# Large buffers moved to multiples of 4 KB, and one projection moved ahead in the tail

## The chip, the core and the metric

The kernel runs on one core of one Trainium2 chip. The core has five engines with an instruction stream each: TensorE (PE, with its weight loads shown as PEld), VectorE (DVE), ScalarE (ACT), GpSimd (POOL) and SyncE (SP), and 16 DMA engines that move data between HBM and the on-chip memory SBUF. SBUF has 128 partitions; a tile takes the same byte range in each of them, so a tile has one start address that holds in every partition. The metric is the device time of one execution in microseconds; less is better.

## What is computed

One step of decoding for a batch of 4: attention over a cache of 4,096 keys and values in 32 heads, a feed-forward block (GEGLU) beside it on the same input, and a gate that mixes the two. All data are float32.

```python
def _A_ref(x, k_cache, v_cache, wq, wo):        # x (4, 1, 512), caches (4, 32, 4096, 128)
    q = (x @ wq).reshape(B, Sq, H, Dh).transpose(0, 2, 1, 3)
    scores = jnp.einsum("bhqd,bhkd->bhqk", q, k_cache) * (Dh ** -0.5)
    p = _softmax(scores, axis=-1)
    o = jnp.einsum("bhqk,bhkd->bhqd", p, v_cache)
    return o.transpose(0, 2, 1, 3).reshape(B, Sq, H * Dh) @ wo      # wo (4096, 512)

def _B_ref(x, w_gate, w_up, w_down):            # (512, 1792), (512, 1792), (1792, 512)
    return (_gelu(x @ w_gate) * (x @ w_up)) @ w_down

g = _sigmoid((x * gate_w).sum(-1, keepdims=True))
return g * a + (1 - g) * b
```

The two caches are 268 MB each; every byte of them is read once.

## The kernel before

**Tiles.** The caches are cut into 64 tiles each (`NT`): tile i holds two heads of one batch, as 128 partitions of 64 keys (or values) of 128 numbers, which is a row of 32,768 bytes in each partition and 4 MB in all. The function `load` issues one DMA from SyncE for a tile (the last V tile in two halves). All large inputs pass through one pool `kv` of five buffers of that size: the two halves of `wq`, the K and V tiles, `w_gate`, `w_up`, and at the end `w_down`, in four parts of 512 rows (the last of 256), each a DMA of its own. `wo` comes in eight pieces of 1 MB into a tile of the pool `work`. A load into a buffer waits until the last reader of what was in it is done; loads are issued in the order of the list `loads`, which puts K of tile i+1 in front of V of tile i, and w_down last.

**The loop.** For each K tile, VectorE multiplies it with the query (L197, `products`) and sums over the 128 numbers (L204, `sums`); a small part of the sums goes to ScalarE (L207). The maximum of a tile's scores goes over TensorE and back (`max_a`, `soft_max`), ScalarE takes the exponentials into `pm`, and TensorE multiplies them with the V tile (L256, `pv`). Each four tiles, `gather` (L265 to L270) collects the result of two heads, `weigh` (L275 to L284) divides it by the sum of the exponentials and turns it into `oT`, and each eight tiles, `project_a` copies it to `ot` (L289) and multiplies it with a piece of `wo` into the accumulator `a_acc`. The feed-forward block runs in between, at tiles 20 and 21; its last product, `ffn_down(j)` with part j of w_down, adds into the accumulator `b_acc`. Both accumulators are written through the helper `project` (L249), 32 matmul instructions for a piece of `wo` or a full part of w_down, 16 for the last part.

**Order and addresses.** The order of the instructions on each engine is the order in which the code stands (`tc.manual_schedule()`); nothing moves them. Pools are placed in SBUF one behind the other in the order in which they are made: `consts`, then `kv`, then `work`. `consts` holds the small tiles that live throughout: the identity `ident`, `ones`, the selectors `sel` and `hsel`, the spread input `xT`, the scratch output `dump` of ScalarE's sums, and others.

**The tail.** Behind the loop, TensorE's order is: the last V tile (`pv(NT - 1)`), ffn_down(0), the last gather, ffn_down(1), the last weigh, ffn_down(2), the last project_a, ffn_down(3). VectorE then weights `a_acc` by the gate (`ta`, L382), adds the weighted `b_acc` (`res`, L385), and SyncE writes the result out (L386).

Of the kernel before, what the change touches and what calls it, by code (L numbers as in the profile page):

```python
# [9 lines left out]
F32 = mybir.dt.float32  # L10
# [7 lines left out]
def tile_gated_mix(ctx: ExitStack, tc: tile.TileContext, x, kc, vc, wq, wo, w_gate, w_up, w_down, gate_w, out):  # L18
    nc = tc.nc
    P = 128  # L20
    B, H, S, D = kc.shape
    DM = x.shape[2]
    F = w_gate.shape[1]
    KC = DM // P
    C4 = DM // 4
    HT = 2
# [3 lines left out]
    NB = 5  # L30
    TW = R * D
    RJ = 4
# [6 lines left out]
    scale = 1.0 / math.sqrt(D)  # L39
    c_gelu = math.sqrt(2.0 / math.pi)  # L40

    consts = ctx.enter_context(tc.tile_pool(name="consts", bufs=1))
    kv = ctx.enter_context(tc.tile_pool(name="kv", bufs=NB))
    work = ctx.enter_context(tc.tile_pool(name="work", bufs=2))
    ps2 = ctx.enter_context(tc.tile_pool(name="ps2", bufs=2, space=PSUM))
    ps1 = ctx.enter_context(tc.tile_pool(name="ps1", bufs=1, space=PSUM))
# [50 lines left out]
    gw = consts.tile([P, KC], F32)  # L97


    ident = consts.tile([P, P], F32)  # L100
    make_identity(nc, ident)
    ones = consts.tile([P, P], F32)
    nc.vector.memset(ones, 1.0)

    sel = consts.tile([P, RJ, B, HT], F32)
    for j in range(RJ):
        nc.vector.tensor_reduce(sel[:, j], ident.rearrange("p (c b m) -> p b m c", c=4, b=B)[:, :, HT * j:HT * (j + 1), :],
                                axis=AX.X, op=OP.add)

    hsel = consts.tile([B * HT, HT, B, 8], F32)  # L110
    for h in range(HT):
        nc.vector.tensor_copy(hsel[:, h], ident[:B * HT, h:B * HT:HT][:, :, None].to_broadcast([B * HT, B, 8]))

# [9 lines left out]
    for c in range(KC):  # L123
        nc.tensor.transpose(xT_ps[:, c, :], x_sb[:, c::KC], ident[:B, :B])

    xT = consts.tile([P, KC, 4, B, 8], F32)
    for c in range(KC):
        nc.vector.tensor_copy(xT[:, c], xT_ps[:, c, None, :, None].to_broadcast([P, 4, B, 8]))
    xT = xT.rearrange("p c j b k -> p c (j b k)")
# [50 lines left out]


    SC = {}
    dump = consts.tile([P, D], F32)
    u = consts.tile([P, 2, FG], F32)

    def parts(i):
# [60 lines left out]
    def project(acc, t, w, start, stop):  # L247
        for c in range(4):
            nc.tensor.matmul(acc[32 * c:32 * c + 32, :], t, w[:, c * C4:(c + 1) * C4], start=start, stop=stop)  # L249
# [23 lines left out]
    def weigh(g):  # L273
        ri = work.tile([B * HT, 1], F32, name="ri")
        nc.vector.reciprocal(ri, OS[g][:, D:])  # L275
        on = work.tile([B * HT, 4, D // 4], F32, name="on")
        nc.vector.tensor_scalar(on, OS[g][:, :D].rearrange("p (k e) -> p e k", e=4), ri, None, op0=OP.mult)  # L277
        w, r = divmod(g, 2)
        if r == 0:
            OT[w] = ps1.tile([P, 4, 32], F32, name="oT")  # L280
        for h in range(HT):
            q = 32 * (HT * r + h)
            for e in range(4):
                nc.tensor.matmul(OT[w][q:q + 32, e, :], on[:, e, :], hsel[:, h].rearrange("p b k -> p (b k)"),  # L284
                                 start=True, stop=True)

    def project_a(w):
        ot = work.tile([P, 4, 32], F32, name="ot")
        nc.scalar.activation(ot, OT[w], AF.Copy)  # L289
        for e in range(4):  # L290
            project(a_acc, ot[:, e, :], WO[w][:, e, :], (w, e) == (0, 0), (w, e) == (H // 4 - 1, 3))
# [34 lines left out]
    def ffn_down(j):  # L326
        w = T["d", 0].rearrange("p (f n) -> p f n", n=DM)
        for f in range(j * FG // P, min((j + 1) * FG, F) // P):
            project(b_acc, hT[:, f, :], w[:, f, :], f == 0, f == F // P - 1)
# [46 lines left out]
    gather(H // HT - 1)  # L376
    ffn_down(1)
    weigh(H // HT - 1)
    ffn_down(2)
    project_a(H // 4 - 1)  # L380
    ta = consts.tile([P, C4], F32)
    nc.vector.tensor_scalar(ta, a_acc, g_cols[:, 0:1], None, op0=OP.mult)  # L382
    ffn_down(3)
# [25 lines left out]
```

## Time and profile before

| | before |
|---|---|
| time, median of 3 runs | 1324.2 us (1324.19 to 1325.61) |
| the profiled execution's own time | 1324.15 us |
| its span, first to last instruction | 1322.4 us |
| mean granted TensorE clock | 0.659 of full speed |
| HBM read | 564.67 MB |
| mean rate over the span | 427 GB/s |

The profile is one execution of the kernel. Its span leaves out what lies ahead of the first and behind the last instruction, here 1.75 us. Its page lists the busy time of each engine, the span in 40 slices of 33 us with the share and rate of the DMA engines, the DMA queues, the chain of work that ended last, and the costliest groups of instructions by line of the code. A row of a group reads: line, engine, operation, output <- input, shapes, count | busy time in us, mean ns of one | idle time of the engine just before, and what ended it. A row of the timeline reads: start in us, length in us, engine, line, operation, with the idle time ahead of it in brackets.

### The profile page before, as it was taken

What the parts mean: (1) busy time and instruction counts of PE and PEld (TensorE: products, weight loads), DVE (VectorE), ACT (ScalarE), POOL (GpSimd) and SP (SyncE); (2) the same over time, 40 slices, a digit from 0 to 9 for tenths busy, and PEclk for the clock granted to TensorE, in tenths of its full rate; (3) what the DMA queues carried; (4) which work ended last, traced back from release to release, by engine and by line L of the source; (5) the groups of instructions that cost most, each with busy time, mean ns of one, the idle gap of its engine ahead of it and who ended that gap; (6) DMA issues with size and microseconds to landing.
All of it is one profiled execution on the core that took longest, in us unless ns stands there. A gap on an engine that the chain in (4) does not pass through costs nothing.

```text
span 1322.4 us, 9351 instructions
## 1 busy us (share of the span) xinstructions
PE 498.6 (38%) x3562; PEld 177.8 (13%) x3562; DVE 1157.2 (88%) x645; ACT 210.4 (16%) x963; POOL 0.7 (0%) x6
## 2 busy tenths in 40 slices
PE   3242433342442453433344243352433343253316
PEld 1011111111110110111111011110101111011102
DVE  1999899989899579998999989899899989999894
ACT  0111111101111111101101101101101101111133
POOL 0000000000000000000000000000000000000000
PEclk9566667666775775766766665766766665666668
DMA  9999999999999999999999999999999999999997
GB/s 411 430 427 429 434 433 431 428 429 433 432 432 429 430 433 431 431 427 433 431 434 432 429 432 431 431 430 431 433 429 431 431 434 431 428 431 430 436 430 315
DMA packets 21096, 565.28 MB, mean 427 GB/s; under 512 B 2472, under 2 KB 2488, under 8 KB 2620
## 3 DMA queue, kind: packets, MB, share of 16 engines
q1 hardware_dynamic: 21052, 564.69, 99.4%
q8 instruction: 28, 0.46, 0.1%
q14 instruction: 16, 0.13, 0.0%
HBM read 564.67 MB, written 0.01 MB: 427 GB/s over the span
## 4 chain that ended last, share of the span: by engine, by line
DMA 71%; DVE 24%; PE 4%; issue 0%; SPq 0%; ACT 0%; DVEq 0%
DMA kv<-in_A_k_cache 51%; DMA kv<-in_A_v_cache 18%; DVE pr L197 13%; DVE sc L204 9%; PE po L256 3%; DMA kv<-in_B_w_down 3%; DVE pa L197 1%; DVE m L230 0%; SPq L59 0%; DVE u L197 0%; PE sm L135 0%; PE b_acc L249 0%; PE q L322 0%; DVE m L223 0%; DVE on L277 0%
## 5 line engine op out<-in xcount | busy, mean ns | idle before, releaser
L256 PE MATMUL po<-kv,pm 128*32 128x512 f32 x2048 | 368.3, 884 | 493.9 <-DMA kv<-in_A_v_cache 488.4
L204 DVE TENSOR_REDUCE sc<-pr 128x20 f32<-128x2560 f32 x190 | 535.8, 2820 | 6.5
L197 DVE TENSOR_TENSOR pr<-kv,qb 128x2560 f32<-128x2560 f32 x190 | 535.3, 2817 | 4.2
L256 PEld LDWEIGHTS po<-kv,pm 128*32 128x32 f32 x2048 | 91.7, 155 | 715.4 <-issue 704.2
L197 DVE TENSOR_TENSOR pa<-kv,qb 128x512 f32<-128x512 f32 x66 | 45.6, 690 | 90.9 <-DMA kv<-in_A_k_cache 90.9
L235 ACT ACTIVATE nb<-sm 128x1 f32<-128x1 f32 x64 | 10.9, 170 | 574.2 <-PE sm L233 574.1
L225 PE MATMUL sm<-ident,m 128*1 128x128 f32 x64 | 19.2, 299 | 199.3 <-DVE m L223 199.3
L207 ACT ACTIVATE dump<-pa 128x128 f32<-128x128 f32 x264 | 81.7, 309 | 10.5 <-DVE pa L197 2.6
L233 PE MATMUL sm<-m,ones 1*64 1x1 f32 x256 | 22.4, 238 | 88.6 <-DVE m L230 88.6
L179 ACT ACTIVATE qb<-q 128x512 f32<-128x512 f32 x16 | 9.6, 597 | 261.1 <-PE q L176 261.1
L207 ACT ACTIVATION_READ_ACCUMULATOR dump<-pa 128x1 f32 x264 | 49.2, 186 | 0.0
L238 ACT ACTIVATE pm<-sc,nb 64x64 f32<-64x64 f32 x128 | 44.6, 348 | 3.0 <-ACT nb L235 0.2
L265 ACT ACTIVATE o<-po 128x512 f32<-128x512 f32 x16 | 9.6, 597 | 194.0 <-PE po L256 194.0
L225 PEld LDWEIGHTS sm<-ident,m 128*1 128x1 f32 x64 | 5.1, 79 | 243.3 <-issue 211.1
L233 PEld LDWEIGHTS sm<-m,ones 1*64 1x64 f32 x256 | 17.0, 182 | 106.4 <-DVE m L230 98.9
L176 PE MATMUL q<-ident,QT 128*64 128x128 f32 x256 | 27.2, 381 | 0.6 <-DVE QT L163 0.6
L238 ACT ACTIVATION_READ_ACCUMULATOR pm<-sc,nb 64x1 f32 x128 | 23.6, 185 | 0.0
L176 PEld LDWEIGHTS q<-ident,QT 128*64 128x64 f32 x256 | 21.5, 194 | 4.4 <-issue 3.0
L268 PE MATMUL sm<-o,sel 128*8 128x128 f32 x128 | 16.6, 273 | 10.7 <-ACT o L265 10.7
L223 DVE TENSOR_REDUCE m<-sc 128x1 f32<-128x64 f32 x64 | 14.1, 220 | 6.6
L230 DVE TENSOR_REDUCE m<-sm 1x2 f32<-1x128 f32 x64 | 17.4, 272 | 1.1 <-PE sm L225 1.1
L268 PEld LDWEIGHTS sm<-o,sel 128*8 128x8 f32 x128 | 10.3, 89 | 26.8 <-ACT o L265 24.9
(56 smaller groups left out, 129.3 us busy)
## 6 DMA issues: line engine op xcount, KB each, us to landing
kv<-in_A_k_cache SPq DMA_DIRECT2D x64, 4096.0 KB, 42.6
kv<-in_A_v_cache SPq DMA_DIRECT2D x63, 4096.0 KB, 34.0
kv<-in_A_wq SPq DMA_DIRECT2D x2, 4096.0 KB, 16.6
wo_sb<-in_A_wo SPq DMA_DIRECT2D x8, 1024.0 KB, 40.7
kv<-in_A_v_cache SPq DMA_DIRECT2D x2, 2048.0 KB, 39.7
kv<-in_B_w_gate SPq DMA_DIRECT2D x1, 3584.0 KB, 44.1
kv<-in_B_w_up SPq DMA_DIRECT2D x1, 3584.0 KB
kv<-in_B_w_down SPq DMA_DIRECT2D x3, 1024.0 KB, 30.4
```

What stands on the lines that cost most here:

```text
L176: nc.tensor.matmul(ps[h * PH:(h + 1) * PH, b, :], QT[:, HT * g + h, b:b + 1].to_broadcast([P, PH]), ident, start=True, stop=True)
L197: nc.vector.tensor_tensor(t, T["k", i].rearrange("p (r d) -> p r d", d=D)[:, r0:r1], QB[g][:, b:b + 1, :].to_broadcast([P, n, D]), op=OP.mult)
L204: nc.vector.tensor_reduce(SC[i][:, r0:r1], t, axis=AX.X, op=OP.add)
L207: nc.scalar.activation(dump, t[:, r - r0, :], AF.Copy, accum_out=SC[i][:, r:r + 1])
L223: nc.vector.tensor_reduce(m1, SC[i], axis=AX.X, op=OP.max)
L225: nc.tensor.transpose(MT[i], m1, ident)
L230: nc.vector.tensor_reduce(m2, MT[i].rearrange("o (h p) -> o h p", h=HT), axis=AX.X, op=OP.max)
L233: nc.tensor.matmul(nbp[h * PH:(h + 1) * PH, :], ones[:1, :PH], m2[:, h:h + 1], start=True, stop=True)
L235: nc.scalar.activation(nb, nbp, AF.Copy, scale=-scale)
L238: nc.scalar.activation(PM[i % 2][:, PZ:].rearrange("p (c m) -> p c m", m=32)[s, :, h:RJ * HT:HT], SC[i][s, :].rearrange("p (c j) -> p c j" ...
L256: nc.tensor.matmul(PO[g % 2][32 * c:32 * c + 32].rearrange("p j d -> p (j d)"), PM[i % 2][:, m0:m0 + 32], T["v", i][:, j * N:(j + 1) * N], ...
L268: nc.tensor.matmul(OS[g][:, :D], sel[:, j].rearrange("p b h -> p (b h)"), o[:, j, :], start=j == 0, stop=j == RJ - 1)
```

## The change

Two things change. Six small tiles (`ident`, `ones`, `sel`, `hsel`, `dump`, `xT`) move from `consts` to a new pool `head`, which is made first, and the pool `kv` is made next, ahead of `consts`. The six tiles take 3,968 bytes of a partition; with 16,384 bytes that are reserved and 128 for the compiler's own constants in front of them, the five buffers of `kv` begin at byte 20,480, which is 5 x 4,096. Before, they began at byte 33,856, which is 8 x 4,096 + 1,088. `work` begins at byte 197,696 in both. And in the tail, the last `project_a` is issued in front of `ffn_down(2)` and no longer behind it.

```diff
+    head = ctx.enter_context(tc.tile_pool(name="head", bufs=1))
+    ident = head.tile([P, P], F32)
+    ones = head.tile([P, P], F32)
+    sel = head.tile([P, RJ, B, HT], F32)
+    hsel = head.tile([B * HT, HT, B, 8], F32)
+    dump = head.tile([P, D], F32)
+    xT = head.tile([P, KC, 4, B, 8], F32)
+    kv = ctx.enter_context(tc.tile_pool(name="kv", bufs=NB))
     consts = ctx.enter_context(tc.tile_pool(name="consts", bufs=1))
-    kv = ctx.enter_context(tc.tile_pool(name="kv", bufs=NB))
     work = ctx.enter_context(tc.tile_pool(name="work", bufs=2))
...
-    ident = consts.tile([P, P], F32)
     make_identity(nc, ident)
-    ones = consts.tile([P, P], F32)
     nc.vector.memset(ones, 1.0)
...
-    sel = consts.tile([P, RJ, B, HT], F32)
-    hsel = consts.tile([B * HT, HT, B, 8], F32)
-    xT = consts.tile([P, KC, 4, B, 8], F32)
-    dump = consts.tile([P, D], F32)
...
     weigh(H // HT - 1)
+    project_a(H // 4 - 1)
     ffn_down(2)
-    project_a(H // 4 - 1)
     ta = consts.tile([P, C4], F32)
     nc.vector.tensor_scalar(ta, a_acc, g_cols[:, 0:1], None, op0=OP.mult)
     ffn_down(3)
```

## The prediction

> **What bounds the kernel now.** I read the page's engine totals and its slices first, then the queues and the chain of waits.
>
> ```profile
> span 1322.4 us, 9351 instructions
> PE 498.6 (38%) x3562; PEld 177.8 (13%) x3562; DVE 1157.2 (88%) x645; ACT 210.4 (16%) x963; POOL 0.7 (0%) x6
> ...
> DMA  9999999999999999999999999999999999999997
> GB/s 411 430 427 429 434 433 431 428 429 433 432 432 429 430 433 431 431 427 433 431 434 432 429 432 431 431 430 431 433 429 431 431 434 431 428 431 430 436 430 315
> ...
> q1 hardware_dynamic: 21052, 564.69, 99.4%
> ...
> DMA 71%; DVE 24%; PE 4%; issue 0%; SPq 0%; ACT 0%; DVEq 0%
> ```
>
> VectorE looks almost full, but the 16 DMA engines are fuller: SyncE's queue takes 99.4% of their span, and only the first and the last slice move clearly less than the others. I then asked for four long windows between start and tail (columns: busy time and count of each engine, TensorE clock, DMA share, GB/s).
>
> ```profile
> 33.00:363.00 330.00, 119.19 (x805) 41.85 (x805) 308.65 (x166) 50.68 (x235) 0.00 (x0) 0.64 1.00 431
> 363.00:693.00 330.00, 127.38 (x874) 44.47 (x874) 289.17 (x155) 48.03 (x217) 0.00 (x0) 0.66 1.00 431
> 693.00:1023.00 330.00, 122.60 (x856) 43.85 (x860) 300.45 (x160) 49.98 (x232) 0.00 (x0) 0.64 1.00 431
> 1023.00:1290.00 267.00, 95.27 (x672) 34.23 (x668) 242.22 (x132) 48.94 (x231) 0.00 (x0) 0.64 1.00 430
> ```
>
> The share is 1.00 and the rate 430 to 431 GB/s in all four, with VectorE busy from 88% (289.17 of 330) to 94% (308.65). So the kernel ends when its bytes have gone through, plus a short tail. The 24% of VectorE in the chain are SyncE's waits for a buffer to come free, and the issues show why they leave no gap:
>
> ```profile
> kv<-in_A_k_cache SPq DMA_DIRECT2D x64, 4096.0 KB, 42.6
> kv<-in_A_v_cache SPq DMA_DIRECT2D x63, 4096.0 KB, 34.0
> kv<-in_A_wq SPq DMA_DIRECT2D x2, 4096.0 KB, 16.6
> ...
> kv<-in_A_v_cache SPq DMA_DIRECT2D x2, 2048.0 KB, 39.7
> kv<-in_B_w_gate SPq DMA_DIRECT2D x1, 3584.0 KB, 44.1
> kv<-in_B_w_up SPq DMA_DIRECT2D x1, 3584.0 KB
> kv<-in_B_w_down SPq DMA_DIRECT2D x3, 1024.0 KB, 30.4
> kv<-in_B_w_down SPq DMA_DIRECT2D x1, 512.0 KB, 34.2
> ```
>
> 4,194,304 bytes at 431 GB/s take 9.7 us, yet a K load lands 42.6 us after its issue and a V load after 34.0: three or four loads always stand in front of it. A shorter transfer is therefore worth its full length at the end, as long as the compute behind it keeps up.
>
> **The change, part by part.** (1) The program's order of instructions is the same on SyncE, VectorE, ScalarE and GpSimd; on TensorE only project_a(7) has changed place. What differs besides is addresses. Before, the five `kv` buffers begin at byte 33,856 of each partition (16,384 reserved, 128 for the compiler's constants, 17,344 for `consts`), which is 8 x 4,096 + 1,088: each row of a load starts 64 bytes beyond a multiple of 256. After, the six small tiles of `head` fill bytes 16,512 to 20,480 and the buffers begin at 5 x 4,096. `work` keeps its addresses in both, so the eight loads of `wo` stay 64 bytes off.
>
> What can a row gain? No row before has an aligned start, so I bound it by what a row costs beside its bytes. Rows of two lengths are in the trace. The tail has the short ones, w_down's rows of 8 KB:
>
> ```profile
> 1311.67 1.08 PE L249 MATMUL b_acc<-kv,hT 128*32 128x128 f32 x32 [0.53 <-DMA kv<-in_B_w_down]
> ...
> 1314.13 1.08 PE L249 MATMUL b_acc<-kv,hT 128*32 128x128 f32 x32 [0.49 <-DMA kv<-in_B_w_down]
> 1315.14 0.59 PE L284 MATMUL oT<-hsel,on 8*32 8x32 f32 x16
> 1316.62 1.08 PE L249 MATMUL b_acc<-kv,hT 128*32 128x128 f32 x32 [0.89 <-DMA kv<-in_B_w_down]
> ```
>
> Parts 0, 1 and 2 release TensorE 2.46 and 2.49 us apart, mean 2.475. A part is 128 rows, 8 for each of 16 engines: 309.4 ns for a row of 8,192 bytes on the engine that ends last. A row of 32,768 bytes goes at 431/16 = 26.94 GB/s: 1,216.4 ns. The difference is 907 ns for 24,576 bytes, 27.1 GB/s for the bytes alone; 8,192 bytes take 302.3 ns at that rate, which leaves about 7.1 ns a row that isn't bytes. (The mean engine stands against the last one here; that makes the 7.1 rough, not its size.)
>
> Loads into `kv`: 64 + 63 + 2 of 4 MB, 2 halves, 2 of 3.5 MB, 4 of w_down: 137, with 8 rows an engine each, 1,096 rows in series. All of the 7.1 ns gone would be 7.8 us; nothing gone is 0. Between the ends I take the share that the offset itself explains: an engine that handles a row from the 256-byte boundary below its start carries 64 bytes in vain. 64 bytes at 26.94 GB/s are 2.4 ns, a third of the 7.1, and 1,096 x 2.4 = 2.6 us. A loss isn't excluded either, since the rate at the new addresses is nowhere to be seen; the spread of the long windows, 1 GB/s of 431, is 0.23% or 3 us, and I take that as the lower end. The value is -2.6, the ends are -7.8 and +3.
>
> The Trainium skill has the rule for that padding: by "DMA: Bandwidth & Descriptors", section "How a descriptor splits into AXI transactions", a descriptor that doesn't start on 256 bytes begins its first transaction at the boundary below, and the unused bytes still cost beats. By the skill's rule -2.6 us would stand, if it holds for the side that writes; but the page words it for what a transaction reads, and here the reads come from HBM, where the change moves nothing: read so, the rule says 0, which is the first rival. It also asks for 256 bytes, so 4 KB as such would bring nothing more. No row here can decide between the two readings.
>
> (2) Cover for the new addresses on the compute side: VectorE's two large groups read from buffers with different offsets (`kv` at 1,088 beyond 4 KB, `pr` at 3,648) and take the same time.
>
> ```profile
> L256 PE MATMUL po<-kv,pm 128*32 128x512 f32 x2048 | 368.3, 884 | 493.9 <-DMA kv<-in_A_v_cache 488.4
> L204 DVE TENSOR_REDUCE sc<-pr 128x20 f32<-128x2560 f32 x190 | 535.8, 2820 | 6.5
> L197 DVE TENSOR_TENSOR pr<-kv,qb 128x2560 f32<-128x2560 f32 x190 | 535.3, 2817 | 4.2
> ...
> L197 DVE TENSOR_TENSOR pa<-kv,qb 128x512 f32<-128x512 f32 x66 | 45.6, 690 | 90.9 <-DMA kv<-in_A_k_cache 90.9
> ```
>
> So I cost them at 0. If `kv` reads did change by 1%, that were 5 us of VectorE, inside the 90.9 us in which it waits for K at the head of a tile; TensorE waits 488.4 us for V. These waits also let compute follow a faster stream: 2.6 us off 64 tiles is 0.04 us a tile. The small tiles' own work and SyncE's issues are the same instructions as before.
>
> (3) project_a(7) in front of ffn_down(2). The rows of the tail, as the chain and the timeline have them:
>
> ```profile
> 1283.16 33.41 DMA kv<-in_B_w_down
> 1316.57 0.04 issue
> 1316.62 1.08 PE b_acc L249 x32
> 1317.70 0.87 PE a_acc L249 x32
> 1318.57 0.48 PE b_acc L249 x16
> 1319.05 0.06 issue
> 1319.11 0.35 DVE res L385
> ```
>
> ```profile
> 1315.76 0.28 ACT L289 ACTIVATE ot<-oT 128x128 f32<-128x128 f32 x1 [3.94 <-PE oT L284]
> ...
> 1318.64 0.35 DVE L382 TENSOR_SCALAR ta<-a_acc,g_cols 128x128 f32<-128x128 f32 x1 [4.44 <-PE a_acc L249]
> 1319.11 0.35 DVE L385 SCALAR_TENSOR_TENSOR res<-b_acc,g_cols,ta 128x128 f32<-128x128 f32 x1
> 1319.49 0.66 SPq L386 DMA_DIRECT2D out<-res  x1
> ```
>
> `ot` is ready at 1316.04, while TensorE stands idle (0.89 us) until w_down's part 2 lets it go at 1316.62. In the new order the 32 matmuls of project_a can start at about 1316.10 and take 1.08 from idle, to 1317.18; part 2 is there by then and takes 0.87 to 1318.05; part 3 takes 0.48 to 1318.53. Before, that end stood at 1319.05: 0.5 us less. Is part 3 there in time? It has half of part 2's bytes, so half of 2.475 us more: it lands at 1316.57 + 1.24 = 1317.8, before 1318.05, with 0.25 to spare. `ta` moves from 1318.64 to about 1317.3 and no longer stands close ahead of `res`, but `res` waits for b_acc anyway, so that adds nothing. The edit adds a wait: ffn_down(2), ffn_down(3), `res` and the output now queue behind project_a's wait for `ot`. The ends: -0.87, all of project_a off the path, and +0.87, all of it in front of a part 2 that is there first (from the point where `ot` comes later than part 2). Since the oT matmuls (1315.14) run behind part 1's, both shift with the same transfers, so I stay near -0.5.
>
> Sum, against the profiled execution's own 1324.15 us (span 1322.4, 1.75 around it; the median of the runs is 1324.2, so the same): 1324.15 - 2.6 - 0.5 = 1321.0 us, which is -0.24%. A difference of 0.2%, 2.65 us, is about what a measurement of this kernel can tell from no change.
>
> **The rivals.** First: the offset costs the stream nothing (writes are cut at the boundary without padding, and the 7.1 ns are something else). Then only the tail moves: 1324.15 - 0.5 = 1323.6, no change. For it: the bytes alone already fit the rows of both lengths, and the best slice of before, 436 GB/s, was reached with the offset. Against it: 7.1 ns a row have to come from somewhere.
>
> Second: the offset is behind the whole fixed cost of a row: 1324.15 - 7.8 - 0.5 = 1315.9, faster. Against it: a row surely costs something for its own start, whatever its address.
>
> Third, slower: rows that all begin at the same place of a 4 KB block meet the engines' reads of other `kv` buffers, all five now at that place too, and the stream loses 1 GB/s, as between the long windows. Its place is every load, its price 3 us: 1324.15 + 3 - 0.5 = 1326.65. It decides from the point where the rate of the windows falls by more than 0.17 GB/s (0.5 of some 1314 us), and is slower by over 0.2% from 1.0 GB/s on. Against it: the five buffers stand a multiple of 32 KB apart before as well, and the rate doesn't fall where VectorE is busiest (431 at 94% and at 88%). The Trainium skill speaks against it too: "SBUF — State Buffer", section "SBUF: two separate sides", says that DMA and engine accesses have ports of their own and cannot slow each other; the windows agree as far as they go.
>
> **How the numbers follow.** The forecast has 0.46; with a row's gain between 1.6 and 3.6 ns its own range is 1319.7 to 1321.9, about four fifths of it below 1321.55, the point of 0.2%. The first rival has 0.31, the second (from 5 ns a row on) 0.10, the third 0.13, most of it over 0.2%. Faster: 0.37 + 0.10 = 0.47. Slower: 0.11. The rest is within 0.2%: 0.31 + 0.09 + 0.02 = 0.42. Both signs are open, so the range runs from 1318.0, on the way to the second rival, to 1326.0, on the way to the third; most of the second and half of the third lie outside, about 0.15, and the unknown sizes take the rest up to 0.2.
>
> **What would show it.** Right: the long windows at 432 GB/s and not 430 to 431; parts 0 to 2 of w_down some 0.02 us closer together; the last K load's matching VectorE products earlier by about 2.5 us; in the tail a_acc's 32 matmuls between oT and part 2, right behind `ot`, and `res` about 2.55 us after `ot` is ready, where it was 3.07 (1319.11 less 1316.04). The first rival shows as the same GB/s in the four windows with the tail alone changed, the second as 433 or more, the third as 429 to 430. The prediction is wrong if VectorE's 2817 ns change, if the windows' share falls below 1.00 (a queue that runs dry), or if part 3 or `ot` becomes the wait that ends last in the tail.

## The result and the profile after

The changed kernel takes 1318.41 us (median, 1318.34 to 1318.88) against 1324.2 us: 5.8 us less, a ratio of 0.9956 with an interval of 0.9945 to 0.9967. Its profiled execution took 1318.34 us. The prediction had 1321.0 and a range from 1318.0 to 1326.0.

The head of the page after, then the four long windows (same columns as before):

```profile
span 1316.6 us, 9351 instructions
PE 495.5 (38%) x3562; PEld 176.0 (13%) x3562; DVE 1157.2 (88%) x645; ACT 210.5 (16%) x963; POOL 0.7 (0%) x6
...
q1 hardware_dynamic: 21052, 564.69, 99.5%
```

```profile
33.00:363.00 330.00, 120.69 (x805) 42.85 (x805) 309.98 (x166) 51.75 (x240) 0.00 (x0) 0.63 1.00 432
363.00:693.00 330.00, 127.55 (x894) 44.42 (x894) 289.28 (x159) 47.54 (x214) 0.00 (x0) 0.67 1.00 433
693.00:1023.00 330.00, 122.71 (x861) 43.31 (x857) 302.57 (x158) 49.44 (x230) 0.00 (x0) 0.65 1.00 433
1023.00:1290.00 267.00, 94.73 (x672) 33.47 (x676) 243.24 (x133) 51.96 (x246) 0.00 (x0) 0.64 1.00 432
```

VectorE's busy time is the same to a tenth of a microsecond, the queue is as full as before, and the same 21,052 packets go through at 432 to 433 GB/s where it was 430 to 431. So most of the gain is in the stream. (The lines of the code stand two further down in the changed kernel: L197 is L199 now.) VectorE's groups by shape show that the products, which read `kv`, take the same 2817 ns at the new addresses, and that the wait for K at the head of a tile became shorter (90.9 us before):

```profile
L206 DVE TENSOR_REDUCE sc<-pr 128x20 f32<-128x2560 f32 x190 | 535.8, 2820 | 6.5
L199 DVE TENSOR_TENSOR pr<-kv,qb 128x2560 f32<-128x2560 f32 x190 | 535.3, 2817 | 4.2
...
L199 DVE TENSOR_TENSOR pa<-kv,qb 128x512 f32<-128x512 f32 x66 | 45.5, 690 | 85.8 <-DMA kv<-in_A_k_cache 85.8
```

The stream can be followed through the tail. VectorE's first product on the last K tile but one, which waits for its load, stands at 1265.25 us; before, it stood at 1270.21 us. These are the two rows:

```profile
1270.21 1.23 DVE L197 TENSOR_TENSOR u<-kv,qb 128x1024 f32<-128x1024 f32 x1 [0.76 <-DMA kv<-in_A_k_cache]
```

```profile
1265.25 1.23 DVE L199 TENSOR_TENSOR u<-kv,qb 128x1024 f32<-128x1024 f32 x1 [0.81 <-DMA kv<-in_A_k_cache]
```

The wait in front of it is nearly the same (0.76 and 0.81 us), the place 4.96 us earlier. The rest is in the tail. These are the rows of TensorE, then of ScalarE and VectorE, and at last the chain of waits:

```profile
1306.41 1.08 PE L251 MATMUL b_acc<-kv,hT 128*32 128x128 f32 x32 [0.54 <-DMA kv<-in_B_w_down]
...
1308.88 1.08 PE L251 MATMUL b_acc<-kv,hT 128*32 128x128 f32 x32 [0.51 <-DMA kv<-in_B_w_down]
1309.89 0.59 PE L286 MATMUL oT<-hsel,on 8*32 8x32 f32 x16
1310.85 1.08 PE L251 MATMUL a_acc<-wo_sb,ot 128*32 128x128 f32 x32 [0.37 <-ACT ot L291]
1311.74 1.49 PE L251 MATMUL b_acc<-kv,hT 128*32 128x128 f32 x48
```

```profile
1310.52 0.28 ACT L291 ACTIVATE ot<-oT 128x128 f32<-128x128 f32 x1 [3.98 <-PE oT L286]
...
1313.31 0.35 DVE L387 SCALAR_TENSOR_TENSOR res<-b_acc,g_cols,ta 128x128 f32<-128x128 f32 x1 [0.96 <-PE b_acc L251]
```

```profile
1277.72 31.11 DMA kv<-in_B_w_down
...
1308.88 1.08 PE b_acc L251 x32
1309.96 0.53 PE oT L286 x16
...
1310.52 0.29 ACT ot L291
...
1310.85 1.08 PE a_acc L251 x32
1311.93 1.35 PE b_acc L251 x48
```

a_acc's matmuls start 0.05 us behind `ot` (ready at 1310.80), and the 48 of parts 2 and 3 follow in one piece, without a wait. `res` starts 2.51 us after `ot` is ready, where it was 3.07. The last load that the chain waits for is w_down's part 1 now (its matmuls start at 1308.88) and no longer part 2; the last wait of TensorE is the 0.37 us for `ot`.

### The profile page after: what moved, and what is told of

Same layout as the page of the kernel before. It is cut to its first block, busy times and chain, and to the rows that moved or that the text cites. A ratio compares the mean times of both kernels' runs of the same rounds, so it can differ in the third digit from the quotient of the medians.

```text
span 1316.6 us, 9351 instructions
## 1 busy us (share of the span) xinstructions
PE 495.5 (38%) x3562; PEld 176.0 (13%) x3562; DVE 1157.2 (88%) x645; ACT 210.5 (16%) x963; POOL 0.7 (0%) x6
## 3 DMA queue, kind: packets, MB, share of 16 engines
q1 hardware_dynamic: 21052, 564.69, 99.5%
## 4 chain that ended last, share of the span: by engine, by line
DMA 67%; DVE 29%; PE 2%; issue 1%; another core or an unknown queue 0%; SPq 0%; ACT 0%; DVEq 0%; ACTq 0%
DMA kv<-in_A_k_cache 54%; DVE pr L199 15%; DVE sc L206 12%; DMA kv<-in_A_v_cache 10%; DMA kv<-in_B_w_down 2%; PE po L258 2%; DVE pa L199 1%; DVE m L232 0%; SPq L67 0%; PE b_acc L251 0%; DVE u L199 0%; DVE on L279 0%; PE sm L138 0%; DVE m L225 0%
## 5 line engine op out<-in xcount | busy, mean ns | idle before, releaser
L199 DVE TENSOR_TENSOR pr<-kv,qb 128x2560 f32<-128x2560 f32 x190 | 535.3, 2817 | 4.2
L199 DVE TENSOR_TENSOR pa<-kv,qb 128x512 f32<-128x512 f32 x66 | 45.5, 690 | 85.8 <-DMA kv<-in_A_k_cache 85.8
L209 ACT ACTIVATE dump<-pa 128x128 f32<-128x128 f32 x264 | 81.7, 309 | 10.4 <-DVE pa L199 2.6
```

Of the source, the lines that this page charges most:

```text
L199: nc.vector.tensor_tensor(t, T["k", i].rearrange("p (r d) -> p r d", d=D)[:, r0:r1], QB[g][:, b:b + 1, :].to_broadcast([P, n, D]), op=OP.mult)
L209: nc.scalar.activation(dump, t[:, r - r0, :], AF.Copy, accum_out=SC[i][:, r:r + 1])
```

## The experiments

**The two halves apart.** The new addresses with the old tail:

```diff
-    project_a(H // 4 - 1)
     ffn_down(2)
+    project_a(H // 4 - 1)
```

> The buffers at a multiple of 4 KB, the old order in the tail. Theory A (the start of a row sets what a row costs on its DMA engine): nearly all of the gain of 5.8 us is here, 1318.9 us, the long windows at 432 to 433 GB/s. Theory T (the tail and the moment at which things meet there made most of it): 1323 us or more, windows at 430 to 431.

Measured: 1318.88 us, ratio 0.9959 [0.9947, 0.9972]. And the old addresses with the new tail:

```diff
+    project_a(H // 4 - 1)
     ffn_down(2)
-    project_a(H // 4 - 1)
```

> The old addresses, project_a(7) in front of ffn_down(2). By the prediction's third part and theory A: 1323.7 us, 0.5 below before. Theory T: 1319 us.

Measured: 1323.59 us, ratio 0.9995 [0.9986, 1.0004], which by its interval can't be told from no change, though its eleven runs (1323.33 to 1323.82) all lie below the lowest of before beside them (1323.93). The medians of the two give 5.2 us and 0.5 us off the 1324.1 of before in these runs, together nearly the whole 5.8. TensorE's rows of the second kernel show where its half microsecond is:

```profile
1314.91 0.59 PE L284 MATMUL oT<-hsel,on 8*32 8x32 f32 x16
1315.86 1.08 PE L249 MATMUL a_acc<-wo_sb,ot 128*32 128x128 f32 x32 [0.37 <-ACT ot L289]
1316.76 1.52 PE L249 MATMUL b_acc<-kv,hT 128*32 128x128 f32 x48
```

The idle time before part 2, 0.89 us in the kernel before, is filled with project_a, and 0.37 us of it are left, in front of `ot`. Theory T is out, theory A stands.

**Alignment or layout?** In the changed kernel, 64 bytes moved ahead of the buffers:

```diff
-    RS = [consts.tile([P, B, HT], F32, name=f"rs{j}") for j in range(2)]
+    RS = [(head if j < 2 else consts).tile([P, B, HT], F32, name=f"rs{j}") for j in range(2)]
```

> The changed kernel with rs0 and rs1 (64 bytes) moved from consts into head: the buffers begin 64 bytes beyond a multiple of 4 KB, all else stays where it is. Theory A: the gain of the addresses is lost, 1323.7 us, windows at 430 to 431 GB/s. Theory L (it is the new layout as such, small tiles in front and consts behind, and not where a row starts): 1318.4 us as in the changed kernel.

Measured: 1323.61 us, ratio 0.9995 [0.9986, 1.0004]: all of the 5.2 us lost by 64 bytes. And in the kernel before, 192 bytes that nothing uses:

```diff
     consts = ctx.enter_context(tc.tile_pool(name="consts", bufs=1))
+    spare = consts.tile([P, 48], F32)
+    nc.gpsimd.memset(spare, 0.0)
```

> The kernel before with 192 unused bytes at the start of consts: the old order of pools and the old tail, but the buffers begin at 133 x 256 (1,280 beyond a multiple of 4 KB), wo's tile at a multiple of 256 too. Theory A in the form 256 bytes: 1318.9 us. Theory A in the form 4 KB: no gain, 1324.2 us. Theory L: 1324.2 us.

Measured: 1318.93 us, ratio 0.9959 [0.9947, 0.9972], the same as the new addresses with the old tail. The first long window of each, the one with 64 bytes first:

```profile
33.00:363.00 330.00, 120.05 (x805) 42.18 (x805) 308.87 (x166) 50.90 (x236) 0.00 (x0) 0.64 1.00 431
```

```profile
33.00:363.00 330.00, 116.32 (x805) 40.86 (x805) 310.13 (x166) 51.69 (x240) 0.00 (x0) 0.65 1.00 432
```

The order of the pools has no part in it, and 4 KB isn't needed: a multiple of 256 bytes (133 x 256, an odd multiple) does the same. A window is a coarse measure here (1 GB/s is 0.23%); the times carry these verdicts.

**What the price goes by.** The same move with other tiles gives other offsets: rs0 alone 32 bytes, pm0 and rs0 2,176 (128 beyond a multiple of 256), both pm tiles 4,288 (192 beyond one). The edit for pm0 and rs0:

```diff
-    PM = [consts.tile([P, PZ + R // RJ * 32], F32, name=f"pm{j}") for j in range(2)]
-    RS = [consts.tile([P, B, HT], F32, name=f"rs{j}") for j in range(2)]
+    PM = [(head if j < 1 else consts).tile([P, PZ + R // RJ * 32], F32, name=f"pm{j}") for j in range(2)]
+    RS = [(head if j < 1 else consts).tile([P, B, HT], F32, name=f"rs{j}") for j in range(2)]
```

> The changed kernel with rs0 moved into head: the buffers begin 32 bytes beyond a multiple of 256. 64 bytes cost 5.2 us (1323.6 against 1318.4). Theory P (the bytes ahead of the start are carried in vain, so the price grows with the offset): half of it, 1321.0 us. Theory C (one cut more a row, the same for every start off 256): 1323.6 us. Theory S (only starts off 64 hurt more, as partial lines): above 1323.6 us.

> The changed kernel with pm0 and rs0 moved into head: the buffers begin 128 bytes beyond a multiple of 256. Theory P: twice the price of 64 bytes, 1328.8 us. Theory C: 1323.6 us. A third possibility, that 128 is aligned enough: 1318.4 us.

> The changed kernel with both pm tiles moved into head: the buffers begin 192 bytes beyond a multiple of 256. Theory P: three times the price of 64 bytes, 1334.0 us. Theory C: 1323.6 us.

Measured: 1324.74 us at 32 bytes, 1323.55 at 128, 1323.52 at 192, beside 1323.61 at 64. Against the changed kernel's 1318.41 these are 6.3, 5.1, 5.1 and 5.2 us. The price doesn't grow with the offset. Theory P, the one the prediction's value stood on, is out; theory C's equal price stands for 64, 128 and 192, and 32 costs 1.1 us more, as theory S had it. The reasons that the two theories give (one cut more a row, partial lines) were not tested by themselves.

**Does each row pay for itself?** The buffers in two pools, so that only some of the five are off by 64 bytes; for one of five:

```diff
-    kv = ctx.enter_context(tc.tile_pool(name="kv", bufs=NB))
+    kv = ctx.enter_context(tc.tile_pool(name="kv", bufs=NB - 1))
+    mid = ctx.enter_context(tc.tile_pool(name="mid", bufs=1))
+    RS = [mid.tile([P, B, HT], F32, name=f"rs{j}") for j in range(2)]
+    kv5 = ctx.enter_context(tc.tile_pool(name="kv5", bufs=1))
...
-        t = T[kind, i] = kv.tile([P, TW], F32, name="kv")
+        t = T[kind, i] = (kv5 if len(T) % NB == NB - 1 else kv).tile([P, TW], F32, name="kv")
...
-    RS = [consts.tile([P, B, HT], F32, name=f"rs{j}") for j in range(2)]
```

> Four of the five buffers at multiples of 4 KB, the fifth 64 bytes beyond one; which load goes to which buffer is as in the changed kernel. If each row pays for its own start: a fifth of 5.2 us, 1319.5 us. If the price is only paid when rows of that kind follow each other for long (something fills up first; in the kernel before, the rows of the first 40 us were not slower than in the changed one): 1318.4 us.

Measured: 1318.50 us: one load in five with the wrong start costs 0.1 us and not 1.0. The other two kernels have three and four such buffers (`NB - 3` and 3, `NB - 4` and 4 in the lines above, with `>=` in place of `==`).

> Three of the five buffers 64 bytes beyond a multiple of 256, so three loads in a row are off and two are not. One of five cost nothing (1318.5 us); five of five cost 5.2 us. If the aligned rows only just made up for the one load between them (each with a quarter of the excess to spare): 1321.0 us. If an aligned row has as much to spare as a row off has in excess: 3 - 2 of 5, 1319.4 us. If it has much more to spare: 1318.4 us.

> Four of the five buffers 64 bytes beyond a multiple of 256. An aligned row with a quarter of the excess to spare: 1322.3 us. With as much to spare as a row off has in excess: 4 - 1 of 5, 1321.5 us. With four times as much or more, so that one load in five empties what four have filled: 1318.4 us.

Measured: 1320.70 us and 1322.28 us, near the first line of each expectation (1321.0 and 1322.3). So part of the excess is bought off by the aligned rows around it: with 1.04 us for each buffer that is off (5.2 / 5), four of five should cost 4.2 and cost 3.9, three should cost 3.1 and cost 2.3; the single aligned buffer has won back 0.3, the two of them 0.8. By the times an aligned row wins back 0.28 (four of five) to 0.40 (three of five) of what a row off costs. The packets put the kernels in the same order. The trace keeps the duration of every DMA packet; for the rows of 32,768 bytes the table has the median, the mean without the some 60 of 16,512 that took 1,260 ns and more, and the share among all:

```
kernel, offset of the kv buffers                    median ns   mean ns   share of all rows at 1213 ns or less
before, 64 bytes                                      1215       1216.7         9%
changed, none                                         1213       1213.0        99%
kernel before with 192 spare bytes, none              1213       1213.0        99%
changed with 64 bytes                                 1215       1216.7        10%
changed with 32 bytes                                 1216       1217.8         3%
changed with 128 bytes                                1216       1216.8        25%
changed with 192 bytes                                1215       1216.7         9%
one buffer of five off by 64                          1213       1213.1        99%
three of five                                         1213       1214.4        65%
four of five                                          1215       1215.6        37%
```

Packets of one engine overlap by 3 to 4 ns in these records, so only differences between kernels count: 3.7 ns a row on the mean engine. The rows of 8,192 bytes and more add up to 1312.1 us an engine before and 1307.7 after, so these durations hold 4.4 of the 5.2 us; the rest is not in them. Rows of 8,192 bytes had 313.5 ns before and 309.4 after, 4.1 ns: the price is one of rows, not of bytes. And 1,024 of these 1,408 are wo's, whose tile stayed 64 bytes off: standing among aligned rows they took 309.1 ns, and 309.0 where the 192 spare bytes align that tile too, so they cost next to nothing, just as one buffer in five.

The order of the rows shows where the price is paid. A load of 4 MB gives each engine eight rows. Sorted by their start, the rows of 32,768 bytes can be put to their loads, 128 to each; the boundaries are rough, as the engines don't run in step. These are the mean durations (ns, again without rows of 1,260 ns and more, and without the first 15 loads), over the whole execution, for each place in the cycle of five buffers and each eighth of a load:

```
three of five off   1st     2nd     3rd     4th     5th     6th     7th     8th
1st aligned load   1216.0  1215.0  1214.0  1213.5  1213.1  1213.0  1213.0  1213.0
2nd aligned load   1213.2  1213.2  1213.0  1213.1  1213.0  1213.0  1213.0  1213.0
1st load off       1213.0  1213.0  1213.1  1213.2  1213.2  1213.5  1213.6  1213.6
2nd load off       1213.9  1213.9  1214.5  1215.1  1215.8  1216.7  1216.9  1216.8
3rd load off       1216.5  1217.0  1216.3  1216.9  1217.1  1217.2  1216.7  1216.2

four of five off    1st     2nd     3rd     4th     5th     6th     7th     8th
aligned load       1216.0  1215.1  1213.9  1213.5  1213.1  1213.0  1213.0  1213.0
1st load off       1213.3  1213.4  1213.3  1213.4  1213.7  1214.4  1215.0  1216.1
2nd load off       1216.3  1216.6  1216.6  1216.8  1217.0  1216.9  1217.0  1216.8
```

The 3rd and 4th load off of the second kernel are like its 2nd. So the price is paid late: after one aligned load some five rows off run like aligned ones before it sets in, after two aligned loads some ten. That is what a reserve does, which aligned rows fill and rows off use up; the aligned rows themselves are no shorter than 1213.0 ns. With one buffer of five off, its rows took 1213.0 to 1213.1 ns throughout.

## Why the prediction was right, and what it had wrong

*What bounds it* held: the share stayed at 1.00, VectorE's 2817 ns didn't move, and the compute followed the faster stream with the same 0.8 us wait at the last K load but one. The time lies in the stated range, but 0.4 us from its lower end and outside the 1319.7 to 1321.9 that the forecast gave itself: it is the room left for the second rival that holds it, not the mechanism that was chosen, and so in part luck.

*Part 1, the addresses*, had the right place and sign, and the wrong size. It took 64 bytes carried in vain, 2.4 ns a row and 2.6 us in all. The addresses alone gave 5.2 us, which over the same 1,096 rows is 4.7 ns, two thirds of the 7.1 ns that were the upper end. (wo's 64 rows an engine, which the count leaves out, became 4.5 ns shorter as well, 0.3 us of the 5.2, although their own start stayed.) The step that failed is the choice between the ends: the padding was chosen because it explains itself by the offset, and no row of before spoke for it. The packets of before did hold a sign of the size: their first rows took 1213.2 ns and the later ones 1216.8, a step of 3.6 ns. The series of offsets refutes it (6.3, 5.2, 5.1 and 5.1 us at 32, 64, 128 and 192 bytes, where padding would cost 2.6, 5.2, 10.4 and 15.6). The rule of the Trainium skill beside it ("DMA: Bandwidth & Descriptors", section "How a descriptor splits into AXI transactions") has the boundary right: 256 bytes and not 4 KB, as the kernel before with 192 spare bytes shows, for writes too, though the page words it for reads. Its count of wasted beats, which grows with the offset, isn't what these writes pay; the measurement decides.

*Part 2, compute at other addresses*, costed at 0, came out at 0. *Part 3, the tail*, was to give 0.5 us and gave 0.5 (1324.10 to 1323.59 alone, 1318.88 to 1318.41 on top of the addresses). Its steps are in the rows: a_acc right behind `ot`, part 2 and part 3 without a wait, 2.51 us from `ot` to `res` where 2.55 was worked out. The fear that part 3 would be late had no cause. The other sign of being wrong, `ot` as the wait that ends last in the tail, did come true: TensorE's last wait is the 0.37 us for `ot`. The sign was drawn wrong, not the step, since the prediction's own working starts a_acc right behind `ot` (1316.04 to 1316.10) and waits for nothing after it.

*The rivals.* The first, no gain from the addresses, is out. The second, the whole fixed cost gone (1315.9), lies as near to the result as the forecast does: the truth was between the two. The third, a slower stream, is out; no window after is below those of before. Of the signs that were named, the windows did show a step, to 432 and 433, between the sign for the forecast (432) and that for the second rival (433 or more); the product on the last K tile but one came 4.96 us earlier and not about 2.5; but the spacing of w_down's parts didn't: 2.46 and 2.49 us before, 2.47 between the first two after. A difference of 0.02 us was too fine a sign; the packets of w_down did become shorter, 313.4 ns before and 309.0 after (one long packet left out), which is 0.035 us for the eight rows of a part.

What stays open is how a row's start comes to cost time. It looks like two steps that run side by side, of which the one that sees the offset is slower than the other with it and a little faster without it, with something between them that holds the reserve. That the price sets in late is seen, in the mixed buffers and in the fast first rows of the kernel before; the two steps and the reserve are argued from it and not seen. The first rows of an aligned load still take up to 1216 ns, which isn't explained either. Nor is it known why 32 bytes cost more than 64.

## What to carry to other kernels

Where a kernel ends when its stream of loads has gone through, start the destination buffers at a multiple of 256 bytes in each partition; here 192 spare bytes in front of a pool gave 0.4%, and no reordering was needed. One buffer of five off cost 0.1 us, three of five 2.3 us, so a few that stand among aligned ones needn't be moved. In a tail that waits for parts of a last load, put work whose inputs are ready earlier in front of the next part: what it is worth is read from when each of the two is ready.

## What was not expected of the hardware

A start 64 bytes off a multiple of 256 costs a row on its engine some 4 ns by the packets (3.7 and 4.1), whether the row is 32,768 or 8,192 bytes long, and only in a long run of such rows; 128 and 192 bytes off cost the same. In the kernel before, the rows that started between 5 and 35 us of the span took 1213.2 ns on the mean, like aligned ones, and those from 60 us on 1216.8; on most engines the change came at about 46 us, when some 36 rows had gone through.
